# Opening phase of a fused recurrence and feed-forward kernel: whole chunks in hand order against single steps in the order of a list schedule

## The chip, the cores and the metric

The kernel runs on one core of a Trainium2 chip. The metric is the device time of one execution in microseconds (us). Every number below compares executions in the undisturbed state; all runs of this study were in it.

The engines: TensorE does the matmuls (PE in the profile, its weight loads PEld), VectorE elementwise work and scans (DVE), ScalarE activations and copies (ACT), GpSimd integer adds and memsets (POOL), SyncE issues the DMA transfers of the one queue used (SP, SPq). The granted clock is the share of TensorE's full clock that the profile shows as let through; 1.00 is full, and matmuls that ran below it are called cold here.

## The reference

Two parts in a row. A gated linear recurrence over 768 tokens, for 4 batches and 8 heads of width 48, and a feed-forward block with a hard-swish gate on the 3072 tokens that result:

```python
for t in range(S):                                     # S = 768, D = 48
    state = alpha[:, :, t, :, None] * state + np.einsum('bhd,bhe->bhde', k[:, :, t], v[:, :, t])
    y[:, :, t] = np.einsum('bhd,bhde->bhe', q[:, :, t], state)
x = y.transpose(0, 2, 1, 3).reshape(B * S, H * D)      # 3072 x 384
h = x @ w_in                                           # 384 x 2048
g = h * np.clip(h + 3.0, 0.0, 6.0) / 6.0
return (g @ w_out).astype(np.float32)                  # 2048 x 384
```

The two weight matrices come in as 64-bit floats. The kernel loads their bits and makes 32-bit floats of them itself.

## The kernel before

The tokens are worked in 24 chunks of 128, and the feed-forward part in groups of two chunks. A chunk's recurrence is turned into matmuls: two scans along the tokens give decays (`R`) and growths (`P`), keys and queries are scaled by them, scores are formed, masked, and multiplied by the values; a running state carries what earlier chunks left.

The weights come in 16 slices (`w.0` to `w.15`), eight of `w_in` and eight of `w_out`. Each is loaded as 0.79 MB of raw bits and decoded: two activations on ScalarE, three instructions on VectorE, one add on GpSimd.

```python
def decode(i):
    ...
    nc.scalar.activation(out=lo.bitcast(I32), in_=lo, func=AF.Copy, scale=2.0**-29)
    nc.scalar.activation(out=dst, in_=hi.bitcast(FP), func=AF.Abs)
    nc.vector.tensor_scalar(dst, dst, LOWEST, HIGHEST, ALU.max, ALU.min)
    nc.vector.tensor_scalar(bits, bits, 3, 0x3FFFFFF8, ALU.logical_shift_left, ALU.bitwise_and)
    nc.vector.scalar_tensor_tensor(hi, hi, 0xC0000000, bits, ALU.bitwise_and, ALU.bitwise_or)
    nc.gpsimd.tensor_tensor(out=dst.bitcast(I32), in0=hi.bitcast(I32), in1=lo.bitcast(I32), op=ALU.add)
```

Raw bits stand in five buffers that are used again, so a load waits until the add of an earlier slice has freed its buffer.

In the traces each engine works through its own list of instructions: VectorE stood 4.32 us at slice 0 while work that did not need the slice lay behind it (the timeline in the prediction). So the order in which the program calls its parts is, engine by engine, the order of execution, but for a few instructions that the scheduler of the compiler pulled forward out of the steady loop. In the steady stage a loop does that. In the opening, where weights are still on their way, it is a list written by hand, of whole parts: `l` loads a chunk, `D` is decays, `S` scaled keys and queries, `s` scores, `o` outputs, `d` a decode, `a` a feed-forward block of six matmul calls (128x256), which the profile records as 12, with its gate, `b` a quarter of an output product.

```python
with tc.manual_schedule():
    run("""l.0 l.1 w.0 w.1 w.2 w.3 l.2 w.4 D.0 S.0 D.1 s.0 d.0 w.5 S.1 o.0 d.1 w.6 s.1 d.2
        w.7 o.1 a.0.0 d.3 a.0.1 l.3 D.2 d.4 a.0.2 S.2 d.5 w.8 a.0.3 s.2 d.6 w.9 a.0.4 o.2
        ... d.15 b.0.3 S.7 b.0.4 l.8 b.0.5 b.0.6 b.0.7""")
combine_w2()
for g in range(2, NG + 1):          # the steady stage
    ...
```

Note `d.0` ahead of `S.1`: VectorE must finish slice 0 before it may touch chunk 1's keys.

## Time and profile before

| | before |
|---|---|
| time, median of 3 runs | 633.17 us |
| profiled run: span / mean granted clock | 631.9 us / 0.972 |
| first feed-forward block starts | 33.77 us |
| last decoded slice (15) ready | 137.5 us |
| third group's third feed-forward block starts | 165.37 us |

The last row is the marker. The time up to the marker is called the opening below. How the opening stands is read from the page's slices, a table of busy time by stretch, the waits and the timeline, which the prediction shows with its lines.

### The profile page before, as it was taken

The page shows a single profiled execution, that of the slowest core. Times are in us where ns is not written, and L with a number is a line of the kernel's source. Part 1 is how long each engine was busy: PE and PEld are TensorE (multiplying, and loading weights), DVE is VectorE, ACT ScalarE, POOL GpSimd, SP SyncE. Part 2 cuts the span into 40 slices and gives each one's busy share as a digit, 9 for nine tenths or more (in the row PEclk, how much of TensorE's full clock was granted, in tenths as well). Part 3 has the DMA queues.
Part 4 walks back from the last instruction along what each step waited for, and adds up shares of the span by engine and source line. Part 5 has one row for each costly group of instructions (what it writes and reads, how often), then busy time and mean ns, then how long its engine had stood idle before and what let it go on. Part 6 is the DMA issues. An engine that isn't in the chain of part 4 may idle for free.

```text
span 631.9 us, 10535 instructions
## 1 busy us (share of the span) xinstructions
PE 598.6 (95%) x4416; PEld 537.2 (85%) x4416; DVE 360.8 (57%) x493; ACT 135.7 (21%) x227; POOL 47.5 (8%) x78
## 2 busy tenths in 40 slices
PE   6587889979899999999999999999999999999998
PEld 5476777746799999999999999999999998999997
DVE  6768675859857746646647747646535424214131
ACT  1353242330012112112112112112112112111110
POOL 2222122040000000000000000000000000000000
PEclk9698997989899999999999999999999999999999
DMA  9994936635325424412312211211000000000000
GB/s 165 200 208 135 175 96 132 110 88 123 93 54 130 99 64 118 107 41 66 80 44 66 65 31 49 65 43 35 20 13 7 8 13 8 7 13 14 6 13 25
DMA packets 90383, 44.73 MB, mean 71 GB/s; under 512 B 54752, under 2 KB 85216, under 8 KB 90336
## 3 DMA queue, kind: packets, MB, share of 16 engines
q1 hardware_dynamic: 90336, 44.06, 31.8%
q8 instruction: 34, 0.56, 0.4%
q14 instruction: 13, 0.11, 0.1%
HBM read 39.32 MB, written 4.72 MB: 70 GB/s over the span
## 4 chain that ended last, share of the span: by engine, by line
PE 86%; DVE 8%; DMA 2%; SPq 1%; issue 1%; ACT 1%; POOL 0%; DVEq 0%; POOLq 0%; ACTq 0%
PE h_ps L382 37%; PE x_ps L471 18%; PE y_ps L471 13%; PE y_ps L369 6%; PE sc_ps L303 4%; PE u_ps L335 3%; PE o_ps L397 2%; PE kb_ps L314 2%; DVE R L268 2%; DMA raw<-in_moe_w_in_dram 2%; DVE P L290 1%; SPq L222 1%; DVE Q L292 1%; PE tr_ps L244 1%; DVE K L288 1%
## 5 line engine op out<-in xcount | busy, mean ns | idle before, releaser
L382 PE MATMUL h_ps<-xT,w 128*128 128x256 f32 x1152 | 269.1, 385 | 0.6 <-ACT xT L374 0.6
L382 PEld LDWEIGHTS h_ps<-xT,w 128*128 128x128 f32 x1152 | 217.0, 193 | 32.9 <-issue 4.4
L386 DVE SCALAR_TENSOR_TENSOR g_sb<-r,h_ps 128x512 f32<-128x512 f32 x96 | 65.7, 685 | 170.0 <-ACT r L385 169.7
L385 ACT ACTIVATE r<-h_ps,half 128x512 f32<-128x512 f32 x96 | 66.0, 688 | 224.0 <-PE h_ps L382 219.5
L471 PE MATMUL x_ps<-rings,g_sb 128*128 128x192 f32 x352 | 60.8, 326 | 0.0
L471 PE MATMUL y_ps<-w,g_sb 128*128 128x192 f32 x352 | 60.8, 326 | 0.0
L471 PEld LDWEIGHTS x_ps<-rings,g_sb 128*128 128x128 f32 x352 | 58.4, 190 | 1.0
L471 PEld LDWEIGHTS y_ps<-w,g_sb 128*128 128x128 f32 x352 | 58.3, 190 | 1.0
L303 PE MATMUL sc_ps<-Q,K 48*128 48x128 f32 x384 | 31.6, 306 | 17.2 <-DVE Q L292 17.2
L303 PEld LDWEIGHTS sc_ps<-Q,K 48*128 48x128 f32 x384 | 26.4, 205 | 23.8 <-issue 10.5
L307 POOL TENSOR_TENSOR t<-t,R 128x384 f32<-128x384 f32 x20 | 17.5, 873 | 371.7 <-DVE t L342 279.1
L268 DVE TENSOR_TENSOR_SCAN R<-t,ones 128x516 f32<-128x516 f32 x24 | 32.3, 1347 | 13.7 <-POOL t L307 9.2
L320 DVE TENSOR_TENSOR A<-sc_ps,mask 128x512 f32<-128x512 f32 x48 | 30.9, 684 | 10.4 <-PE sc_ps L303 10.4
L290 DVE TENSOR_TENSOR_SCAN P<-t 128x516 f32<-128x516 f32 x24 | 30.8, 1282 | 0.4
L471 PE MATMUL x_ps<-w,g_sb 128*128 128x192 f32 x176 | 30.4, 326 | 0.0
L471 PE MATMUL x_ps<-rings,s 128*128 128x192 f32 x176 | 30.4, 326 | 0.0
L471 PE MATMUL y_ps<-w,s 128*128 128x192 f32 x176 | 30.4, 326 | 0.0
L374 ACT COPY xT<-y_ps 128x384 f32<-128x384 f32 x24 | 11.5, 479 | 87.8 <-PE y_ps L369 87.7
L471 PEld LDWEIGHTS x_ps<-w,g_sb 128*128 128x128 f32 x176 | 29.2, 190 | 0.8
L471 PEld LDWEIGHTS x_ps<-rings,s 128*128 128x128 f32 x176 | 29.2, 190 | 0.5
L471 PEld LDWEIGHTS y_ps<-w,s 128*128 128x128 f32 x176 | 29.2, 190 | 0.5
L369 PE MATMUL y_ps<-A,t 128*32 128x128 f32 x768 | 27.2, 283 | 1.9 <-DVE A L320 1.9
(72 smaller groups left out, 496.5 us busy)
## 6 DMA issues: line engine op xcount, KB each, us to landing
raw<-in_moe_w_out_dram SPq DMA_DIRECT2D x8, 768.0 KB, 4.4
t<-in_v_dram SPq DMA_DIRECT2D x48, 96.0 KB, 2.8
raw<-in_moe_w_in_dram SPq DMA_DIRECT2D x24, 192.0 KB, 7.1
out_dram<-o SPq DMA_DIRECT2D x44, 96.0 KB, 1.7
aq<-in_alpha_dram SPq DMA_DIRECT2D x32, 96.0 KB, 2.4
raw<-in_k_dram SPq DMA_DIRECT2D x32, 96.0 KB, 2.2
raw<-in_q_dram SPq DMA_DIRECT2D x32, 96.0 KB, 2.2
aq<-in_alpha_dram SPq DMA_DIRECT2D x32, 80.0 KB, 2.3
```

The costliest lines, as they stand in the source:

```text
L268: nc.vector.tensor_tensor_scan(out=reverse(R, n - 1, n), data0=reverse(ax, n, n), data1=reverse(ones, n, n), initial=0.0, op0=ALU.mult, op ...
L290: nc.vector.tensor_tensor_scan(out=P, data0=ax[:, 0:n], data1=ic, initial=0.0, op0=ALU.mult, op1=ALU.add)
L303: nc.tensor.matmul(sc[h % 2][:, h // 2], K[r, h // 2], Q_t[j][r, h // 2], start=True, stop=True)
L307: nc.gpsimd.tensor_tensor(out=st[j % 2], in0=sm[j % 2], in1=R_t[j][:, :, 0:1].to_broadcast([C, NP, 2 * D]), op=ALU.mult)
L314: nc.tensor.transpose(kp[:, p], K[:, p], ident)
L320: nc.vector.tensor_tensor(out=A[:, NP * o : NP * (o + 1)], in0=sc[o], in1=mask.unsqueeze(1).to_broadcast([C, NP, C]), op=ALU.mult)
L335: nc.tensor.matmul(u[:, p], kb[:, p], both, start=True, stop=True)
L369: nc.tensor.matmul(y[32 * i : 32 * i + 32, kk], lhsT, rhs, start=(n < 4), stop=(n >= len(mms) - 4), skip_group_check=True)
L382: nc.tensor.matmul(h_ps[:, i], w1[:, kk, (f0 + i) * C : (f0 + i + 1) * C], xT_t[g][:, kk], start=(kk == 0), stop=(kk == KT - 1))
L385: nc.scalar.activation(out=r, in_=h_ps, func=AF.Relu, bias=half, scale=1.0 / 6.0)
L386: nc.vector.scalar_tensor_tensor(out=gs[g % 2][:, f0 : f0 + 2], in0=r, scalar=1.0, in1=h_ps, op0=ALU.min, op1=ALU.mult)
L471: nc.tensor.matmul(to[g], lhs[:, f], rhs[:, f], start=(first and f == 0), stop=(last and f == HF - 1), skip_group_check=True)
```

## The change

Intent: let no engine stand at an instruction whose input is late while later instructions of its list could run. Each part is split into single steps, one engine's work each, and the opening's list is no longer written by hand but taken from a list schedule that was made offline; so is the queue's order, in which the loads come one after another as before. In the steady loop the steps are called in the old order of parts.

```diff
-    def decode(i):
+    def round_low(i):
+        nc.scalar.activation(out=lo.bitcast(I32), in_=lo, func=AF.Copy, scale=2.0**-29)
+    def magnitude(i):
+        nc.scalar.activation(out=dst, in_=hi.bitcast(FP), func=AF.Abs)
+    def join_high(i):                       # the three VectorE instructions
...
+    def add_low(i):                         # the add on GpSimd
...
-            {"l": load, "w": load_weight, "d": decode, "D": decays, "S": scaled, "s": scores,
-             "o": outputs, "a": f1, "b": f2}[name](*at)
+    steps = {"la": ..., "lk": ..., "lq": ..., "lv": ..., "w": load_weight,
+        "d1": round_low, "d2": magnitude, "d3": join_high, "d4": add_low,
+        "ta": ..., "tk": ..., "tq": ..., "ca": place_alpha, "r": decay, "p": growth,
+        "k": ..., "q": ..., "sc": scores, "m": masked, "kb": k_by_token, "ck": keep_k,
+        "st": decayed_state, "u": update, "sm": next_state, "yi": within, "yx": across,
+        "cy": keep_x, "f": ff1, "fr": gate, "fg": hidden, "b": ff2, "bo": store, "x": combine_w2}
...
-        run("""l.0 l.1 w.0 w.1 w.2 w.3 l.2 w.4 D.0 S.0 D.1 s.0 d.0 w.5 S.1 o.0 d.1 w.6 s.1 d.2
...
+        run("""la.0 lk.0 lq.0 ta.0 lv.0 ca.0 la.1 tk.0 r.0 lk.1 tq.0 k.0 lq.1 p.0 ta.1 lv.1 q.0
+            ca.1 w.0 tk.1 r.1 sc.0 tq.1 k.1 m.0 kb.0 ck.0 u.0 p.1 w.1 yi.0 sm.0 q.1 cy.0 st.1
+            d1.0 sc.1 d2.0 m.1 kb.1 w.2 ck.1 u.1 d3.0 yi.1 d1.1 yx.1 d2.1 sm.1 d4.0 w.3 cy.1
+            d3.1 f.0.0 d1.2 d2.2 d4.1 la.2 fr.0.0 fg.0.0 f.0.1 lk.2 d3.2 d1.3 lq.2 d2.3 lv.2
...
+            cy.6 tq.7 sm.6 b.1.0 q.7 st.7 sc.7 b.1.1 m.7 kb.7 b.1.2 ck.7 u.7 b.1.3 sm.7 yi.7
+            bo.1 x.0 yx.7 x.1 cy.7 x.2 x.3 la.8 lk.8 lq.8 lv.8""")
-    combine_w2()
```

Three things besides order: chunk 7's scores and outputs and the four combinations of `w_out` (`x.0` to `x.3`) move from behind the list into its end, and the first two feed-forward blocks of the third group now come behind the list. The work itself is unchanged.

## The prediction

> **What bounds the kernel now.** I read the page's slices first, to see whether one engine sets the whole span or only part of it.
>
> ```profile
> PE   6587889979899999999999999999999999999998
> ...
> DVE  6768675859857746646647747646535424214131
> ...
> PEclk9698997989899999999999999999999999999999
> DMA  9994936635325424412312211211000000000000
> ```
>
> Each digit is 15.8 us. From the twelfth slice on TensorE is at 9 without a break, at full clock. Before that no row is: TensorE runs at 5 to 9 with a reduced clock, VectorE at 5 to 9, and the DMA engines are full only in the first three slices. So there are two stages: an opening with no single bound, and a steady stage bound by TensorE. A table of busy time by stretch puts the border at 165 us, where the third feed-forward block of the third group starts.
>
> ```profile
> core 0: us, PE busy (x) PEld busy (x) DVE busy (x) ACT busy (x) POOL busy (x), PEclk, DMA share, GB/s
> 0.00:33.77 33.77, 20.69 (x169) 17.04 (x169) 22.72 (x39) 9.64 (x13) 9.70 (x32) 0.80 1.15 185
> 33.77:65.80 32.03, 26.45 (x201) 22.74 (x202) 24.78 (x34) 14.32 (x20) 6.65 (x5) 0.95 0.78 166
> 65.80:104.46 38.66, 33.99 (x329) 29.08 (x328) 25.01 (x38) 12.63 (x19) 8.23 (x7) 0.91 0.69 150
> 104.46:137.55 33.09, 28.02 (x166) 21.15 (x165) 23.99 (x32) 14.15 (x20) 9.38 (x10) 0.98 0.46 98
> 137.55:165.37 27.82, 25.94 (x161) 18.96 (x161) 23.74 (x27) 1.86 (x4) 1.44 (x10) 0.87 0.30 74
> 165.37:632.00 466.63, 463.53 (x3400) 428.24 (x3396) 240.57 (x325) 83.12 (x151) 12.12 (x14) 1.00 0.19 47
> ```
>
> The last row reads 463.5 of 466.6 us TensorE busy, clock 1.00: a rearranged opening can't shorten that. Everything that can be won lies in the 165.4 us above it. There TensorE is busy 135.1 us, but matmuls that wait inside or run at a low clock count as busy, so I ask how much work that was at the full-clock durations of the later stages: 64 feed-forward records of 128x384 at 0.325 us (5.2 us per 16) are 20.8 us; sixteen blocks of twelve 128x256 records at 2.59 are 41.4; per chunk twelve transposes 1.31, scores 1.0, key transposes 0.44, state update 0.7, outputs 0.95 and 0.72, which over the eight chunks (some lack a part) are 37.3. Sum 99.5 us. VectorE has nearly as much: the groups of the opening add up to 16 decoded slices x (0.64+0.66+0.96) = 36 us, eight chunks' scans, products, masks and state adds 50 us, 16 gate products 11 us, the four w2 combinations 7, the combinations of g 3.6, memsets 3.5: 111 us. The queue has to bring eight chunks and 16 slices of 0.79 MB, 18.9 MB. Its first 49 us, full, bring four chunks and eight slices, 9.4 MB, so about 98 us in all. Three resources of about 100 us each, and the opening takes 165: that is a matter of order, and the waits say which.
>
> ```profile
> PE sc_ps L303 <- DVE Q L292: 17.2, 6, 6.1
> DVE g_sb L386 <- ACT r L385: 17.8, 7, 4.8
> DVE w L189 <- ACT w L188: 13.4, 8, 4.3
> DVE K L288 <- PE tr_ps L244: 5.6, 1, 5.6
> SPq L169 <- POOL w L195: 39.6, 8, 8.4
> ```
>
> Columns: who waited for whom, us in total, times, longest. Scores waited 17.2 us for the scaled queries, VectorE 17.8 us for gates on ScalarE and 13.4 us for a slice's magnitude, and the DMA queue 39.6 us for the add on GpSimd that frees a raw buffer. The timeline shows one such case whole.
>
> ```profile
> 16.29 0.91 ACT L185 ACTIVATE raw<-raw 128x768 int32<-128x768 uint32 x1 [1.86 <-DMA raw<-in_moe_w_in_dram]
> 18.06 0.69 DVE L189 TENSOR_SCALAR w<-w 128x768 f32<-128x768 f32 x1 [4.32 <-ACT w L188]
> ...
> 20.39 0.68 DVE L288 TENSOR_TENSOR K<-tr_ps,R 128x512 f32<-128x512 f32 x1
> ...
> 24.20 2.08 PE L303 MATMUL sc_ps<-Q,K 48*128 48x128 f32 x16 [6.14 <-DVE Q L292]
> ...
> 33.77 1.59 PE L382 MATMUL h_ps<-xT,w 128*128 128x256 f32 x6 [0.60 <-ACT xT L374]
> ```
>
> VectorE, working in list order, sat 4.32 us until slice 0 had come and been touched by ScalarE, then did its three steps, and only at 20.39 began chunk 1's keys, which do not need the slice. TensorE's scores of chunk 1 waited 6.14 us behind that, and the first feed-forward block came at 33.77.
>
> **What the Trainium skill says.** "Perfetto Trace Analysis", section "Optimization Strategy": where a kernel has regimes with different most-contended engines, interleaving the regimes may help. That is the change's intent, and the table above shows such regimes. "TensorE: Matmul & The Clock Gate", section "What's actually happening": after about 3.4 us idle the array runs at half clock until it has been busy about as long. The trace agrees: the sixteen score records after the 6.14 us wait took 2.08 us, those at 64 us on a warm array 1.16. So a wait removed in the opening also pays in shorter matmuls after it. "SBUF — State Buffer", section "Who interferes with whom": a VectorE instruction with two SBUF inputs contends with a GpSimd instruction that reads SBUF, and the later one is blocked whole. Here:
>
> ```profile
> 90.41 1.46 POOL L195 TENSOR_TENSOR w<-raw 128x768 int32<-128x768 int32 x1 [5.92 <-DVE raw L193]
> 90.91 2.05 DVE L268 TENSOR_TENSOR_SCAN R<-t,ones 128x516 f32<-128x516 f32 x1
> ```
>
> A scan took 2.05 us beside the decode's add and 1.24 elsewhere in the trace. Sixteen adds of 1.47 us remain after the change, so this cost is moved, not removed; the VectorE sum above includes it.
>
> **The change part by part.** No work is removed or added: the decode's five instructions, the loads, matmuls and copies are the same. I compared the compiled orders of both kernels.
> 1. Queue: every entry up to chunk 5's loads is identical. After that four alpha quarter loads of chunk 8 and three of chunk 9 no longer stand ahead of slice 11 and chunk 6. Slices 11 and 12 come before chunk 6.
> 2. VectorE: chunk 1's keys, masks, scan, queries all stand before the first decode. By the old durations: chunk 0 as before to 9.8 us, chunk 1's decay from 10.7, keys at 12, mask of chunk 0 to 15.3, scan and queries to about 19, scores 21, mask 22.3, then slice 0 decoded to 24.6, add 26. So the first feed-forward block starts at about 26 in place of 33.8: 7 to 8 us earlier.
> 3. Later, each chunk's five VectorE steps are spread between gates and decodes, and its scores and outputs between single feed-forward blocks, so that the gate's and the magnitude's ScalarE time (0.69 and 1.8 us) lies under other VectorE work.
> 4. Chunk 7's scores and outputs and the w2 combinations, which stood in the steady loop, are now in the list. In exchange the old order had pulled forward two feed-forward blocks and two products of the steady stage, 2x2.59 + 2x2.60 = 10.4 us. At equal work the old opening therefore ended at 165.4 - 10.4 = 155.0.
>
> The sum goes by the last slice, 15: it gates the fourth quarter of the old-form output product, which before started at 137.55, after waiting for the add. In the new order VectorE does 91 us of the opening's work before slice 15 is joined (111 less 3.5 of memsets and less 16.1 that stands behind it: chunk 7 but for its copy, the last steps of chunk 6, the w2 combinations), beginning at 5.9. Idle that I see no way round in the first two chunks is 4.4 us (16.4 us elapsed from 5.9 to 22.3 with 12 of work), and the add is 1.5: 5.9+91+4.4+1.5 = 103 us at best, against 137.55. The DMA gives the same floor: slice 15 landed at about 98, plus 1.8 ScalarE, 2.2 VectorE, 1.5 GpSimd, is 103.5. TensorE has 81 us of full-clock work before that point, with perhaps 8 of cold clock and 4 before the first chunk: 93. With all three within 10% some waiting is sure. I take 10 us, under a third of the 34 us that the old order lost against the same floor; this is my choice, not a reading. So slice 15 is ready at 113. Behind it TensorE has 18.8 us (half a quarter 1.3, four quarters 10.3, chunk 6's and 7's last steps 7.2), with 2 us for chunk 7's chain: 134. The rest is 466.5 + 10.4 = 476.9 in the span; the measured time was 1.3 us above the span. 134 + 476.9 + 1.3 = 612 us, 21 less than 633.17.
>
> **The rivals.** A: the static list doesn't survive real latencies; a queue entry that waits for its buffer holds up all behind it, as 39.6 us of queue waits show today, and slice 15 comes at 122 or later. Then the gain is 10 to 12 us, time 621 to 623. For it: all three resources are near their limit. Against it: in the new list each decode stands early enough that I find the buffer free when the queue comes to it, for slices 8 to 15, by 0 to 7 us. B: VectorE becomes the bound outright, with collisions with GpSimd growing because both are busier. Each costs about 1 us; five more would make 617. C: the gain is given back after the opening, because chunks 8 and 9 and the combinations meet there and the products wait for t[2]. Against it: TensorE has five blocks, about 13 us, between the last output quarter and the first product that needs t[2], VectorE needs 5 for it. I give it 1 to 2 us. D: the list is as good as its floor, slice 15 at 105: 604.
>
> **Range and chances.** D with a little loss gives the low end, 603; A the high end, 622. Two per cent faster is below 620.5, which needs 13 of the 34 us. Only A or a worse case misses that: faster 0.81, same 0.17, slower 0.02, because the steady stage's work and order are unchanged.
>
> **What would show it.** The first 128x256 block near 26 us instead of 33.8; scores waiting for queries well under 17 us in the opening; queue waits on the GpSimd add well under 39.6 us; VectorE over 80% busy between 20 and 110 us; TensorE's clock in the opening nearer 1; the last 477 us unchanged. I am wrong if slice 15's add ends after 122 us, if the time after the opening grows by over 4 us, or if the first feed-forward block is not earlier.

## The result, and the profile after

| | before | after |
|---|---|---|
| time, median of 4 runs | 633.88 us (632.0 to 634.62) | 610.06 us (608.35 to 610.89) |
| ratio, 95% interval | | 0.9625 (0.9594 to 0.9656) |
| span / mean granted clock | 631.9 / 0.972 | 608.1 / 1.000 |
| first feed-forward block starts | 33.77 | 26.65 |
| slice 15 ready | 137.5 | 111.6 |
| marker | 165.37 | 142.51 |

A ratio is the mean time of one kernel's fast runs over that of the other's of the same rounds, so it is not quite the ratio of the medians. The kernel is 3.75% faster. Of the 23.8 us between the two spans, 22.9 lie before the marker.

The page's slices of the kernel after, 15.2 us each:

```profile
PE   6778999999999999999999999999999999999998
...
DVE  7698979869877577467467477357446224115141
...
PEclk9999999999999999999999999999999999999999
DMA  9999998324354243132131131130000000000000
```

TensorE is at 9 from the fifth slice on, where it was from the twelfth, the granted clock is never below 9, and the DMA engines, full for three slices before, are full for six. VectorE, at 5 to 9 in its first twelve slices before, is at 6 to 9 in them now. The same in numbers, for 20 to 110 us, first of the kernel before, then of the one after. Columns: stretch, its length, then busy us of PE, PEld, DVE, ACT, POOL with their instructions, granted clock, DMA share, GB/s.

```profile
20.00:110.00 90.00, 74.28 (x638) 63.61 (x639) 63.64 (x91) 34.02 (x50) 21.16 (x17) 0.87 0.77 156
```

```profile
20.00:110.00 90.00, 80.82 (x692) 64.90 (x690) 78.89 (x110) 44.77 (x64) 28.30 (x23) 1.00 0.95 190
```

VectorE went from 71% (63.64 of 90) to 88% (78.89 of 90). The stretches of the kernel after:

```profile
26.65:54.57 27.92, 22.86 (x170) 18.61 (x171) 23.17 (x33) 14.15 (x21) 10.23 (x7) 1.00 1.00 192
54.57:90.00 35.43, 33.71 (x297) 28.48 (x297) 31.27 (x46) 16.77 (x25) 11.63 (x9) 1.00 0.98 210
...
111.76:132.10 20.34, 20.34 (x174) 13.70 (x173) 11.96 (x16) 2.56 (x5) 2.22 (x11) 1.00 0.31 77
132.10:608.00 475.90, 473.06 (x3452) 437.36 (x3452) 256.73 (x342) 84.77 (x154) 12.45 (x14) 1.00 0.19 47
```

Behind the first feed-forward block TensorE still stands idle for 5.1 us (22.86 busy of 27.92); from 54.57 to 90 it is busy 33.7 of 35.4 us and VectorE 31.3, so little is left there. Once slice 15 is in (111.76), TensorE is busy 20.34 of 20.34 us to the third group's first block, and 473.1 of the 475.9 us from there to the end.

The waits of the opening (0 to 140 us; the prediction's lines of the kernel before are for 0 to 165): who waited for whom, us in total, times, longest. First those of the engines, then one of the queue.

```profile
PE h_ps L408 <- POOL w L201: 7.7, 6, 2.0
...
PE sc_ps L314 <- DVE q L306: 1.1, 1, 1.1
...
DVE g_sb L418 <- ACT r L413: 3.2, 5, 1.4
...
DVE w L192 <- ACT w L185: 2.3, 2, 2.1
```

```profile
SPq L169 <- POOL w L201: 18.5, 5, 6.2
```

The scores' wait for queries fell from 17.2 to 1.1 us, VectorE's for gates from 17.8 to 3.2, for magnitudes from 13.4 to 2.3. New at the head is TensorE's wait for decoded slices (`h_ps` for the add on GpSimd), 7.7 us in six pieces: the decode now sets the pace there; that it is VectorE's part of it is tested below. The queue still waits for adds, 18.5 us against 39.6.

The timeline of the front (start, length, engine, instruction, and in brackets the idle time before it):

```profile
12.04 0.66 DVE L306 TENSOR_TENSOR k<-tk_ps,R 128x512 f32<-128x512 f32 x1
...
18.71 0.69 DVE L306 TENSOR_TENSOR q<-tq_ps,P 128x512 f32<-128x512 f32 x1
...
22.60 0.68 DVE L192 TENSOR_SCALAR w<-w 128x768 f32<-128x768 f32 x1
```

```profile
26.65 2.86 PE L408 MATMUL h_ps<-xT,w 128*128 128x256 f32 x12 [1.23 <-POOL w L201]
```

Chunk 1's keys stand at 12.04 in place of 20.39, all of the chunk is out of VectorE's way when slice 0's decode begins at 22.60, and the first feed-forward block starts 7.1 us earlier. And two lines of the last slice:

```profile
110.18 1.46 POOL L201 TENSOR_TENSOR w<-raw 128x768 int32<-128x768 int32 x1 [7.73 <-DVE raw L196]
110.47 2.27 DVE L282 TENSOR_TENSOR_SCAN R<-t,ones 128x516 f32<-128x516 f32 x1
```

The add frees slice 15 at 111.6, and a scan that was issued 0.3 us behind it takes 2.27 us in place of 1.22. The collision between GpSimd and VectorE is there as before.

### The profile page after: what moved, and what is told of

Same layout as the page of the kernel before. It is cut to its first block, busy times and chain, and to the rows that moved or that the text cites. A ratio compares the mean times of both kernels' runs of the same rounds, so it can differ in the third digit from the quotient of the medians.

```text
span 608.1 us, 10549 instructions
## 1 busy us (share of the span) xinstructions
PE 588.9 (97%) x4416; PEld 527.5 (87%) x4416; DVE 362.1 (60%) x493; ACT 135.3 (22%) x227; POOL 49.8 (8%) x78
## 4 chain that ended last, share of the span: by engine, by line
PE 81%; DVE 0%; ACT 0%; issue 0%
PE h_ps L408 35%; PE x_ps L503 19%; PE y_ps L503 14%; PE sc_ps L314 3%; PE y_ps L378 3%; PE o_ps L430 2%; PE u_ps L356 2%; PE y_ps L388 2%; PE kb_ps L331 1%; DVE raw L196 0%; DVE q L306 0%; PE tq_ps L255 0%; ACT o L509 0%
## 5 line engine op out<-in xcount | busy, mean ns | idle before, releaser
L408 PE MATMUL h_ps<-xT,w 128*128 128x256 f32 x1152 | 265.8, 382 | 7.7 <-POOL w L201 7.7
L408 PEld LDWEIGHTS h_ps<-xT,w 128*128 128x128 f32 x1152 | 214.0, 190 | 39.5 <-POOL w L201 9.6
L314 PEld LDWEIGHTS sc_ps<-q,k 48*128 48x128 f32 x384 | 24.7, 197 | 7.9 <-issue 5.9
L314 PE MATMUL sc_ps<-q,k 48*128 48x128 f32 x384 | 29.4, 295 | 1.1 <-DVE q L306 1.1
```

Source lines behind the costliest of these rows:

```text
L314: nc.tensor.matmul(sc[h % 2][:, h // 2], K_t[j][r, h // 2], Q_t[j][r, h // 2], start=True, stop=True)
L408: nc.tensor.matmul(h[:, f], w1[:, kk, o : o + C], xT_t[g][:, kk], start=(kk == 0), stop=(kk == KT - 1))
```

## The experiments

Twelve kernels ran. The kernel before ran beside each call, with medians of 633.57, 633.65 and 633.61 us, so times of different calls may be set side by side to about 0.2%. The changed kernel was not run again in these calls, so it is tied to them through the kernel before. All outputs are right. The theory under test: the gain is VectorE's, freed of waits in the front and the middle, with VectorE the engine that binds the new opening. The rivals: the front gains nothing because the middle has slack; the gain is the clock, not the waits; the queue binds.

| kernel | us, median | ratio to before (95%) | marker in its profile |
|---|---|---|---|
| before | 633.6 | | 165.37 |
| split_old | 632.16 | 0.9982 (0.9960 to 1.0004) | 164.07 |
| front_new | 628.49 | 0.9921 (0.9897 to 0.9944) | 160.93 |
| warm_old | 625.98 | 0.9875 (0.9839 to 0.9911) | 158.41 |
| mid_old | 621.35 | 0.9813 (0.9789 to 0.9837) | 153.74 |
| plus_dve | 619.52 | 0.9776 (0.9756 to 0.9796) | 152.65 |
| plus_pe | 616.19 | 0.9715 (0.9674 to 0.9755) | 150.96 |
| front_old | 615.73 | 0.9724 (0.9704 to 0.9744) | 148.04 |
| after | 610.06 | 0.9625 (0.9594 to 0.9656) | 142.51 |
| plus_dma | 609.79 | 0.9629 (0.9611 to 0.9647) | 142.46 |
| late_comb | 609.29 | 0.9618 (0.9597 to 0.9638) | 141.06 |
| best | 606.91 | 0.9577 (0.9558 to 0.9595) | 138.44 |
| minus_dve | 605.09 | 0.9550 (0.9533 to 0.9568) | 137.40 |
| no_add | 604.94 | 0.9562 (0.9532 to 0.9591) | 136.73 |

Between the marker and the end of the span each profile has 465.4 to 466.6 us (late_comb 467.4). So what an experiment does to the opening is what it does to the time.

### Control: the split alone (split_old)

The changed kernel's code, with its list replaced by the old list, each part written out as its steps:

```diff
-        run("""la.0 lk.0 lq.0 ta.0 lv.0 ca.0 la.1 tk.0 r.0 lk.1 tq.0 k.0 lq.1 p.0 ta.1 lv.1 q.0
...
+        run("""la.0 lk.0 lq.0 lv.0 la.1 lk.1 lq.1 lv.1 w.0 w.1 w.2 w.3 la.2 lk.2 lq.2 lv.2 w.4 ta.0
+            ca.0 r.0 tk.0 tq.0 k.0 p.0 q.0 ta.1 ca.1 r.1 sc.0 st.0 kb.0 ck.0 m.0 d1.0 d2.0 d3.0
+            d4.0 w.5 tk.1 tq.1 k.1 p.1 q.1 u.0 sm.0 yi.0 yx.0 cy.0 d1.1 d2.1 d3.1 d4.1 w.6 sc.1
...
+    run('x.0 x.1 x.2 x.3')
```

> The changed kernel's code with single steps, but the steps put back in the old order (loads, decodes and chunk steps in their old blocks, chunk 7's scores and outputs and the w2 combinations back in the steady loop). If the gain comes from the order alone: the old time, 633 us within 2, third group's first feed-forward block and all else at the old places, first 128x256 block at 33.8. If splitting itself (other tiles' names, other bank allocation, keys before the scan in the steady loop) gives part of it: below 630.

Measured: 632.16 us, the interval includes 1, and its waits are the old ones (scores for queries 18.1 us, queue for the add 41.1). The split by itself does nothing that can be told from noise; the order does it. This kernel is the base for single parts of the order.

### New front, old rest (front_new)

The new list up to the first feed-forward block `f.0.0`, then the old list for what is left:

```diff
             d3.1 f.0.0
-            d1.2 d2.2 d4.1 la.2 fr.0.0 fg.0.0 f.0.1 lk.2 d3.2 d1.3 lq.2 d2.3 lv.2 ...
+            la.2 lk.2 lq.2 lv.2 w.4 st.0 w.5 yx.0 d4.1 w.6 d1.2 d2.2 d3.2 d4.2 w.7
+            fr.0.0 fg.0.0 d1.3 d2.3 d3.3 d4.3 f.0.1 fr.0.1 fg.0.1 la.3 lk.3 lq.3 lv.3 ta.2 ca.2 ...
```

> New order up to the first feed-forward block, old order for all that follows. Theory that a front gain passes through, since VectorE has more work queued than time: the first 128x256 block at 26.7 and the whole 7 us faster, 626 to 627. Rival, that the loads absorb it (the old middle waits for slices 5 to 7 which land no earlier): block at 26.7, but the total only 0 to 2 us faster, 631 to 633.

Measured: the first block starts at 25.92, 7.4 us before the control's 33.33, and 5.1 of it by the medians (3.7 against the control) reach the end. That lies between the two branches of the expectation: half to two thirds of the front passes through, so the rival that the rest swallows all of it falls, and so does a full pass.

### Old front, new rest (front_old)

The counterpart: the old list up to the first two blocks, then the new list.

```diff
-            d1.0 sc.1 d2.0 m.1 kb.1 w.2 ck.1 u.1 d3.0 yi.1 d1.1 yx.1 d2.1 sm.1 d4.0 ...
+            d4.0 w.5 tk.1 tq.1 k.1 p.1 q.1 u.0 sm.0 yi.0 yx.0 cy.0 d1.1 d2.1 d3.1 d4.1 w.6 sc.1 ...
+            fg.0.0 f.0.1 d1.3 d2.3 ta.2 fr.0.1 tk.2 ca.2 fg.0.1 tq.2 d3.3 f.0.2 ...   (new from here)
```

> Old order up to the first feed-forward block, new order after it. Pass-through: 7 us slower than the changed kernel, 617. Absorption by the loads: 610 to 612, because the new middle has the DMA engines full until 110 us anyway and the 7 us fall into its waits for slices.

Measured: 615.73, so 5.7 us above the changed kernel, with the first block at 33.46. Both ways the front is worth 4 to 6 us. The other three quarters of the gain are behind it.

### New front and end, old middle (mid_old)

The new list to `f.0.0`, the old one up to slice 15's add, the new one after it:

```diff
             (front_new's list up to)   ca.7 r.7 d1.15 d2.15 d3.15 d4.15
-            b.0.3 bo.0 tk.7 tq.7 k.7 p.7 q.7 b.1.0 la.8 lk.8 lq.8 lv.8 b.1.1 b.1.2 b.1.3 bo.1
+            tk.7 b.0.3 k.7 p.7 bo.0 tq.7 b.1.0 q.7 st.7 sc.7
+            b.1.1 m.7 kb.7 b.1.2 ck.7 u.7 b.1.3 sm.7 yi.7 bo.1 x.0 yx.7 x.1 cy.7 x.2 x.3 la.8 ...
```

> New order up to the first feed-forward block, old order from there until the last slice is decoded, new order for the rest (chunk 7, last output quarters, combinations). If the parts add up (front 7, middle 13 to 14, tail 2 to 3 of the 23 us): 623 to 624. If the middle is worth nearly all: 628 or more.

Measured: 621.35, below both branches of the expectation, 11.3 us above the changed kernel and 7.1 below front_new. That makes a chain in which one part is made new at a time: 633.57, front 628.49 (5.1), end 621.35 (7.1), middle 610.06 (11.3). Replaced in this order, the middle is the largest part, but the end was not expected to be worth so much. (In their profiles the first blocks of front_new, mid_old and the changed kernel start at 25.92, 25.01 and 26.65 although the front is the same; the last section says what is probably behind it. So the shares are good to about 1 us, by estimate.) The timelines of the two show why. First front_new, with the old end, then mid_old, with the new one; both lines of each are TensorE's, the first the half quarter that waited for slice 15, the second the block at the marker.

```profile
133.10 2.93 PE L430 MATMUL o_ps<-w,g_sb 128*128 128x384 f32 x4 [3.57 <-POOL w L201]
...
160.93 3.67 PE L408 MATMUL h_ps<-xT,w 128*128 128x256 f32 x12
```

```profile
131.90 1.56 PE L430 MATMUL o_ps<-w,g_sb 128*128 128x384 f32 x4 [2.24 <-POOL w L201]
...
153.74 2.75 PE L408 MATMUL h_ps<-xT,w 128*128 128x256 f32 x12
```

From that half quarter to the marker front_new takes 27.8 us and mid_old 21.8. In front_new TensorE waits 3.57 us and then runs cold: the same four matmuls take 2.93 us in place of 1.56, the granted clock of the next 6.9 us is 0.59. Further on it waits 1.9 us for chunk 7's masks and the block at the marker takes 3.67 in place of 2.75. In mid_old the wait is 2.24 us, the clock stays at 1.00, and the steps of chunk 7 lie between output quarters, so nothing waits.

Two parts of the change have no run of their own. The queue's order is the same in the old and the new list, entry by entry; what differs in the compiled kernels is a few quarter loads of chunks 8 and 9 that the old order had earlier, so its share should be small, but it was not taken apart. And one engine's new order beside the old order of the others was not run: the two lists differ in which of two engines waits for the other, so mixing them by engine could close a circle of waits.

### VectorE heavier and lighter (plus_dve, minus_dve)

The first `tensor_scalar` of each decode done twice, and not at all (it clamps very small and very large magnitudes):

```diff
+        nc.vector.tensor_scalar(dst, dst, LOWEST, HIGHEST, ALU.max, ALU.min)   # plus_dve: a second time
-        nc.vector.tensor_scalar(dst, dst, LOWEST, HIGHEST, ALU.max, ALU.min)   # minus_dve: left out
```

> The changed kernel with the decode's clamp (VectorE, 0.56 to 0.69 us) issued twice per slice: 16 x 0.58 = 9.3 us more VectorE work, same result. If VectorE bounds the new opening: 7 to 9 us slower, 617 to 619. If the three resources share it as I predicted (floors 103, 103.5 and 93): 3 to 6 us. If the loads bound it: 0 to 2 us.

> The changed kernel without the clamp (right for these weights, wrong for zero ones): 9.3 us less VectorE work. If VectorE bounds: 6 to 9 us faster, 601 to 604. If the loads' floor is as high: 0 to 2 us faster. Shared: 2 to 4.

Measured: 619.52 (+9.5) and 605.09 (-5.0). The added sixteen stand in the record with a mean of 625 ns, 10.0 us, so each us more on VectorE costs nearly a whole us, and each us less gives about half, between two branches of the expectation. TensorE's waits for decoded slices move with it; first plus_dve, then minus_dve, where the changed kernel has 7.7:

```profile
PE h_ps L409 <- POOL w L202: 9.9, 6, 2.5
```

```profile
PE h_ps L407 <- POOL w L200: 3.4, 4, 1.3
```

So VectorE's part of the decode is on the path that binds the new opening. Two things are not told apart: a `tensor_scalar` more or less is VectorE time, and it is also a longer or shorter way from a slice's load to its use. Since relief gives back only half, another limit should lie close under it. The profile of the changed kernel shows how close: between the first feed-forward block and slice 15 (26.65 to 111.76) TensorE is idle for 7.9 us in all (77.2 busy of 85.1), 5.1 of them before 54.57. In that stretch a faster VectorE can win no more than those. The next experiment asks for TensorE's share.

### TensorE heavier (plus_pe)

Transposes of chunks 2 to 7 written twice, into the same place:

```diff
-        for p in range(NP):
+        for p in [p for p in range(NP) for _ in range(2 if j >= 2 else 1)]:   # ta, tk, tq; kb alike
```

> The changed kernel with the transposes of chunks 2 to 7 (input and key) issued twice: 72+16 instructions of 0.11 us, 9.7 us more TensorE work, same result. If TensorE has room in the opening: 0 to 3 us slower. If it is as bound as the others: 5 to 9 us.

Measured: a median of 616.19 (+6.1), in two levels, 614.0 twice and 618.3 twice. By the difference of the four groups of transposes the addition is 10.6 us busy, so TensorE is close to binding too: 0.4 to 0.8 us per us. The levels themselves are taken up in the last section.

### The queue heavier (plus_dma)

Ten more transfers of 0.2 MB each between the opening's loads, from the inputs to rows of the output, both in DRAM; the rows are written again later:

```diff
+            if name != "q" and 2 <= j < 7:
+                i = NCH - 10 + 2 * (j - 2) + (name == "k")
+                nc.sync.dma_start(out=out[i * C : (i + 1) * C, :].rearrange("s (h d) -> s h d", h=H),
+                                  in_=src.rearrange("h s d -> s h d"))
```

> The changed kernel with ten more copies of 196 KB in 192-byte pieces beside the loads of alpha and k of chunks 2 to 6 (to rows of the output that are written over at the end): 1.97 MB, about 10 us of the queue at the 192 GB/s of the opening. If the loads bound the opening: 7 to 12 us slower. If the queue has the 7 us of room that I worked out for slices 11 to 15: 0 to 4.

Measured: 609.79, no cost. The queue took the 2 MB, about 10 us at the 190 GB/s of the changed kernel's opening, out of its own waits: for the add it waits 8.0 us in place of 18.5. The same stretch of the changed kernel and of this one (columns as above):

```profile
49.00:98.00 49.00, 47.28 (x446) 39.45 (x446) 42.73 (x63) 24.48 (x35) 17.08 (x12) 1.00 0.96 203
```

```profile
49.00:98.00 49.00, 47.27 (x447) 39.42 (x446) 42.77 (x63) 24.40 (x35) 15.88 (x11) 1.00 1.03 234
```

A DMA share of 0.96 was not a full queue: it moved 234 GB/s when asked, and the columns of PE, DVE and ACT did not change. The loads are not a bound of the new opening. One reserve: this profile has an earlier front (first block at 24.92 in place of 26.65) and yet the same marker, so a cost of about 1 us may hide behind it.

### The old order, kept warm (warm_old)

The rival says that the clock, not the waits, made the old opening slow. The control, with 53 matmuls on constants put ahead of the scores of chunks 1 to 6, written to a place that the scores overwrite:

```diff
+        for i in range({1: 14, 2: 14, 3: 5, 4: 5, 5: 12, 6: 3}.get(j, 0)):
+            nc.tensor.matmul(sc[0][:, i % NP], ident, mask, start=True, stop=True)
```

> The old order (as in the control) with idle matmuls before the scores of chunks 1 to 6 (14, 14, 5, 5, 12, 3 of them, into the bank that the scores overwrite), where TensorE waited for the queries: only to keep its clock up. The cold matmuls on the old chain of waits cost about 6.5 us over their warm durations. If a good part of the 23 us was the clock: 4 to 7 us faster than the control, 625 to 628, granted clock over 0.99. If the order alone matters: 631 to 634.

Measured: 625.98, 6.2 us below the control, though it does more work; the mean clock is 0.991 in place of 0.978. The scores of chunk 1, first in the control, then here:

```profile
24.27 2.08 PE L314 MATMUL sc_ps<-q,k 48*128 48x128 f32 x16 [7.06 <-DVE q L306]
```

```profile
24.02 1.16 PE L316 MATMUL sc_ps<-q,k 48*128 48x128 f32 x16 [2.27 <-DVE q L306]
```

They start at the same time, since they need the queries, but take 1.16 us in place of 2.08. So some 6 us of the old opening's loss went through the clock. By the profiles, which differ by 5.7 us at the marker, 1.1 were won by the first feed-forward block (32.20 in place of 33.33), another 3.8 by the half quarter behind slice 15 (132.11 in place of 137.06), and only 0.7 between there and the marker, where the array still turned cold (the four matmuls took 2.93 us behind a wait of 2.72). The split between clock and waiting is not a clean one: the dummy matmuls take TensorE time.

### Without the add on GpSimd (no_add)

The collisions could cost more than they show. The joined high bits are written straight to the weight, the low bits are left out (a less exact weight):

```diff
-        nc.vector.scalar_tensor_tensor(hi, hi, 0xC0000000, bits, ALU.bitwise_and, ALU.bitwise_or)
+        nc.vector.scalar_tensor_tensor(bits, hi, 0xC0000000, bits, ALU.bitwise_and, ALU.bitwise_or)
-        nc.gpsimd.tensor_tensor(out=dst.bitcast(I32), in0=hi.bitcast(I32), in1=lo.bitcast(I32), op=ALU.add)
```

> The changed kernel without GpSimd's add of a slice's low part; VectorE's third step writes the slice itself (weights cut to 20 bits of mantissa, so a slightly wrong result on purpose). It takes away the collisions of scans with the add (5.5 us of VectorE time in the opening) and 1.5 us between decode and use. If collisions matter like other VectorE time (5 us for 9.3 without the clamp): 3 to 4 us faster, 606 to 607. If the step on the way to the feed-forward matters as well: 6 to 9 us, 601 to 604. If neither: 609 to 611.

Measured: 604.94, 5.1 us less. The scans of the first 140 us, in the changed kernel and here (after the bar: busy us, mean ns):

```profile
L282 DVE TENSOR_TENSOR_SCAN R<-t,ones 128x516 f32<-128x516 f32 x10 | 14.0, 1412 | 2.4 <-ACT t L273 2.4
```

```profile
L281 DVE TENSOR_TENSOR_SCAN R<-t,ones 128x516 f32<-128x516 f32 x10 | 12.2, 1225 | 2.5 <-ACT t L272 2.4
```

The lengthening is gone with the add. The slowed instructions of the changed kernel's opening add up to about 5.5 us over their lengths alone (four scans, two `tensor_scalar`, one combination of `g`, 0.6 to 1.0 each). But the add's own 1.5 us per slice also left the chain, so what of the 5.1 us is collision and what is chain stays open.

### Combinations held back (late_comb)

In the changed kernel VectorE has two combinations of `g` (three instructions, 4.4 us) ahead of slice 15's join, since the scheduler pulled them forward from the steady loop. Here they are named in the list, behind chunk 7's masks:

```diff
-            ... sc.7 b.1.1 m.7 kb.7 b.1.2 ck.7 ...
+            ... sc.7 b.1.1 m.7 cg.0 cg.1 kb.7 b.1.2 ck.7 ...
-            if i < 3:
+            if (g > 2 and i < 2) or i == 2:
                 combine_g(g - 1, i)
```

> The changed kernel with the three first combinations of the gated products of group 1 (4.4 us on VectorE, which the scheduler put between gates and the last two slices) held back to chunk 7's mask, where VectorE idles. At the rate of the run without the clamp (5.0 us for 9.3) 2 to 3 us faster, 607 to 608, slice 15 ready 4 us earlier. If they lay in VectorE's idle time anyway: 610.

Measured: 609.29, not to be told from 610.06; a miss. Slice 15's add starts at 106.76, 3.4 us earlier, but TensorE comes to that quarter only at 110.24, 2.0 us after the slice is ready, so 1.5 us are won at the marker, and the profiled run loses them again behind the last matmul. It shows the other limit once more. In the changed kernel the two arrive together: the slice at 111.64, TensorE at 111.69, after 1.1 us of waiting for chunk 6's queries, which stand behind the join on VectorE.

### A version that beats both (best)

late_comb, with `w_in`'s slices laid out so that a slice is one contiguous run of 768 per partition in place of 3 rows of 256:

```diff
-    w1 = consts.tile([C, KT, DF], FP, tag="w1")
+    w1 = consts.tile([C, DF // 256, KT, 256], FP, tag="w1")
-            return w1[:, :, i * n : (i + 1) * n]
+            return w1[:, i]
-                nc.tensor.matmul(h[:, f], w1[:, kk, o : o + C], xT_t[g][:, kk], ...
+                nc.tensor.matmul(h[:, f], w1[:, i, kk, f * C : (f + 1) * C], xT_t[g][:, kk], ...
```

> As the run before, and the decoded first weight laid out so that each slice is one contiguous row of 768: the clamp and shift on it should take 0.56 us as those on the second weight do, in place of 0.69, 16 x 0.13 = 2.1 us less VectorE work before 60 us. 3 to 4 us faster than the changed kernel in all, 606 to 607. If the shape isn't what made them 0.69: same as the run before.

Measured: 606.91 (605.83 to 607.22), below every run of late_comb beside it (608.37 to 610.28) and 3.1 us below the changed kernel. The shift-and-mask instruction, in the changed kernel and here:

```profile
L194 DVE TENSOR_SCALAR w<-w 128x768 uint32<-128x768 uint32 x16 | 10.0, 625 | 0.5
```

```profile
L193 DVE TENSOR_SCALAR w<-w 128x768 uint32<-128x768 uint32 x16 | 9.0, 560 | 0.6
```

In the changed kernel the mean of 625 is half 690 (the slices of 3 rows) and half 560 (those of `w_out`). The Trainium skill, "Vector Engine (DVE) Microarchitecture Reference", section "5.1 Performance modes — why throughput varies by op and dtype", says that with two ports each takes one half of the outermost dimension, and that of an odd count the first port takes the larger part. With 3 rows of 256 that is 512 elements in place of 384; by the 0.96 GHz that "VectorE: DVE Perf Modes", section "Specifications", gives, an estimate of 128 / 0.96 = 133 ns more. The trace has 130. Two instructions by eight slices by 0.13 is 2.1 us less VectorE work, and 2.4 us lie between the medians of late_comb and best. That all of it is the layout's is not shown: minus_dve gave back only half of what it took from VectorE, and in the profiles best also had the earlier front (first block at 24.80 in place of 26.36).

## Why the prediction was right

The kernel was predicted at 612 us and took 610.06, within the range. By its own steps:

- **The first block at about 26.** Right: 26.65. But the 7 us of it were worth 4 to 6 at the end (front_new, front_old). The prediction carried no such share, since it summed VectorE's work to slice 15 instead, and that sum holds.
- **Slice 15 at 113.** Right: 111.6, and term by term. VectorE is busy 88.5 us between 5.87 and 109.95 (predicted 91); it is idle 5.9 us up to the first decode (4.4) and 9.7 us behind it. The last term was predicted as 10 by choice, not from a reading, so that it fits so well is luck.
- **The floor shared by three resources.** This step failed for one of them. "The DMA gives the same floor", 103.5 us, took the rate of the first 49 us as the most that the queue can do. The opening then ran at 190 GB/s, at 210 between 54.57 and 90, and at 234 with plus_dma's transfers in it, at no cost. VectorE costs 0.95 us per us added, TensorE 0.4 to 0.8, the queue nothing that could be seen. The time came out right because VectorE's floor stood at the same place. TensorE's term was a little small: 81 us of work and 8 of cold clock before slice 15, where the profile has it busy 95.5 us up to 111.76.
- **The buffer is free when the queue comes.** Wrong as told: the queue still waited 18.5 us for adds; slice 15's load was issued at 94.15, just when slice 12's add (92.66 to 94.13) had freed its buffer. Harmless: ScalarE had finished with slice 15 at 102.3, and VectorE began it only at 106.8; plus_dma says the same. So rival A was right in what happens and wrong in what it costs.
- **The end behind slice 15: 18.8 + 2.** Right: 20.3 us, TensorE without a gap.
- **The rest, 476.9 in the span.** Right: 475.9. Rival C, gain given back later, did not happen. The 1.3 us from span to time is a slip: it sets a median beside the span of another run. Runs with both show 2.0 us before and 1.8 after, a difference of 0.5 to 0.7 us that has no weight here. And the low end of the range, 603, lies below rival D's own 604, though it is called D "with a little loss".
- **The clock.** It was named as a side effect; only TensorE's floor, which was not the highest, had a term for it. Keeping the old order warm gave 6.2 us, so by that run about a quarter of the gain may go by that way. Only 0.7 us of these fall behind slice 15, where the old end is cold by itself (0.59 for 6.9 us in front_new); that part comes on top. The prediction did not see this share because it took the old end as measured, with its cold stretches, and summed the new one from full-clock durations; the gain was in its total, not in its reasons.
- **Rival B, collisions.** They stayed at about what the old sum included: the slowed instructions add up to 5.0 us in the opening before and 5.5 after. Taking their cause away together with the add gave 5.1 us. So they are no new loss; how much of the bound they are stays open.

## What to carry to other kernels

When several engines are near their limit, sum the work of each up to the last thing that all wait for, add the idle time at the start that no order removes, and test the sum by giving each engine some more work: the one that makes the end move is the bound, and a busy share of 0.96 on a queue need not be. Giving an engine less work tells how far away the next limit is: here half of the relief was lost to it. Splitting parts into steps is worth nothing by itself; it is worth what the order then lets pass ahead of a late input, and in this kernel more than three quarters of that lay in the middle and the end, not in the front to which a first look at the timeline points. A wait on TensorE costs more than its length if the array turns cold in it (four matmuls took 2.93 us in place of 1.56 behind a wait of 3.57), so read the matmuls behind a wait in the timeline and price it with them.

## What the Trainium skill lacked or had wrong

- "TensorE: Matmul & The Clock Gate", section "What's actually happening", lets the array turn cold after an idle window of about 3.4 us. The prediction's 6.14 us wait agrees. But in warm_old four matmuls were cold (2.93 us) behind a wait of 2.72, and in front_new the block at the marker ran at a clock of 0.77 behind two waits of 0.98 and 0.90; mid_old stayed at 1.00 behind one of 2.24. So a wait shorter than the window does not mean a warm array here.
- The same section puts the ramp at under 1% of a typical span, for one ramp; a later section of the page has a kernel that cools again and again while it waits for loads. Neither prices waits for another engine: warm_old's 6.2 us are 1.0% of the span, but nearly 4% of an opening of 164 us.
- The same section says that the window is free-running and the ramp varies from run to run. The runs here agree, and put a size on what that does further on, which the page has not: among kernels with the same front the eight state-update matmuls of chunk 0, at 15.8 us, took 1.13 us (best) or 2.02 (changed kernel), and those of chunk 1 still took 2.02 at 23.42 in a run of plus_pe; the first feed-forward block started at 24.80, 26.65 and 29.28. That is probably, though no run isolates it, what made plus_pe's two levels 4.3 us apart. The profile's clock column reads 1.00 in these first 20 us all the same.
- "Perfetto Trace Analysis", section "Identifying the Most-Contended Engine", ranks engines by how busy they are, and warns against doing so with the DMA's share. The warning held: a share of 0.95 cost nothing for 2 MB more. What it lacks is a way to tell which of several engines at about 90% binds: from 20 to 110 us TensorE was busy 90% and VectorE 88%, and each us added cost 0.95 us on VectorE and 0.4 to 0.8 on TensorE.
- "Vector Engine (DVE) Microarchitecture Reference", section 5.1, has the rule for odd row counts but no price: 690 against 560 ns for a `tensor_scalar` of 768 elements as 3 rows of 256 or in one run.
